# Where late rows of y are computed and moved in a one-core attention and mode-mixing kernel

## The chip, the cores and the metric

The kernel runs on one core of one Trainium2 chip. The metric is device time in microseconds (us) of a whole execution. The engines that matter are TensorE (PE, matrix products), VectorE (DVE), ScalarE (ACT), GpSimd (POOL) and SyncE (SP), which issues transfers. Each takes its instructions in a fixed order, and the engines wait for each other by semaphores. TensorE writes to PSUM, from where VectorE and ScalarE read.

## The reference

For eight batches and eight heads of 576 positions by 64, causal attention with a forget gate is computed. Its output, as rows of 512 features, is x. A real Fourier transform of x along the sequence is cut to 64 modes, each mode is multiplied by its own complex 512 x 512 matrix, and the inverse transform gives y. With u = x + y the result is u + relu(u w_ch).

```python
X = np.fft.rfft(x, axis=1)
Yr = np.einsum('bmd,mde->bme', Xr, w_r) - np.einsum('bmd,mde->bme', Xi, w_i)
Yi = np.einsum('bmd,mde->bme', Xr, w_i) + np.einsum('bmd,mde->bme', Xi, w_r)
y = np.fft.irfft(Y, n=S, axis=1)
u = x + y
return (u + np.maximum(u @ w_ch, 0.0)).astype(np.float32)
```

The mode matrices are 64 x 2 x 512 x 512 values in float32, far more bytes than the rest of the inputs.

## The kernel before

The features are split into four chunks of 128 (`dc`). In the first part of the kernel the attention of all heads of a chunk is computed batch by batch, its output goes into `x_all`, and a product with a basis gives the modes of x (`XT3`). Beside it the mode matrices are loaded, by transfers that POOL issues at line 86, as tiles of four modes: `wb` holds both matrices of four modes for one chunk, 1 MB as they arrive, in a ring of nine buffers. There are 4 x 16 = 64 mode tiles. `emit_modes(n)` multiplies one with the modes of x (32 matmuls of 16 columns at line 111) and adds the result to the sum over chunks in VectorE (line 122, or 126 for the last chunk).

For the last chunk the tiles are taken in a turned order, so that the modes 0 to 15 come last, as tiles 60 to 63 (`GL` is 4). The other 48 modes end in `YT`, in which the places of modes 0 to 15 are zero; the late 16 modes end in `YTl`. Only the last tile's load is cut into two halves of modes, each with a transfer for either matrix: four transfers of 256 KB instead of two of 512 KB. Its matmuls take the first half's modes first.

What the output needs of a batch are two matrices in `yy`: the mode rows transposed to lie with modes on partitions (index 0), and the same times `w_ch` (index 1). Each has 128 rows, a real and an imaginary one for each mode; rows 0 to 31 are the late modes. `emit_y(b)` computes both for one batch from `YT`: four matmuls of 512 columns into `pyw` (line 596) and four transposes into `yp` (line 606), which ScalarE (603) and VectorE (609) copy to `yy`. It writes the late rows too, as zeros. `emit_late(q4)` does the same for the late modes of four batches at once, from `YTl`, into one PSUM tile `pl` (lines 644 and 648): the four batches' late rows stand under each other, 32 each, and eight copies of 32 rows (lines 658 and 659, VectorE and ScalarE) move them to rows 0 to 31 of `yy`. The two copies of a batch read the same `pl`, and are made to follow each other.

Outputs are written by 24 jobs: for each batch, rows 0 to 255, rows 256 to 511, and rows 512 to 575. `emit_x` opens a job with products with the identity matrix, which put x (`pu`, line 667) and x times w_ch (`pz`, line 672) into PSUM. `emit_out` adds the inverse transform by products with the basis `BI` (line 684, two for each of `pu` and `pz`, one in a job of 64 rows), then ends the job in one of two ways. A job of rows 256 to 511, the first job and the last one copy `pu` on ScalarE (L700) and take the maximum and add on VectorE (L701). The others leave x out of `pu`, add it on VectorE (L694), take the maximum on ScalarE (L697) and add on POOL (L698). Then SP issues the store (L707, or L705 for 64 rows).

`pu`, `pz`, `pl` and the last mode tile's sum all use the pool `psZ`: four PSUM buffers of two banks. A buffer is free again when the last reader of its tile is done.

The order before the last tile is set by a loop that takes tiles up to 62, and after the tiles 60, 61 and 62 emits two, two and four batches of y. Then `emit_x` of the first job, tile 63, `emit_late(0)` and the jobs follow in program order, with `emit_late(1)` in front of job 3. A scheduler then sets each engine's order from priorities and free buffers, so that neighbours in the program can change places: in the built program the copies of `pl` already stand one by one between the evictions of the first outputs.

## Time and profile before

| | us |
|---|---|
| median of 7 runs | 469.97 |
| the runs | 468.49, 468.57, 468.59, 469.97, 470.22, 470.35, 470.75 |
| profiled execution | 468.59 |
| its span, first to last instruction | 466.6 |
| TensorE busy | 324.7 (70%) |
| VectorE busy | 251.0 (54%) |
| ScalarE busy | 250.8 (54%) |
| GpSimd busy | 123.5 (26%) |
| weight transfers (POOL's queue), share of 16 engines | 86.9% |
| mean granted TensorE clock | 0.802 |

Times in the profile are counted from the first instruction. "L111" is a line of the kernel file. An arrow in square brackets names what ended an engine's idle time before an instruction. The chain of work that ended last is followed back from the last instruction, at each step to what released it. A stage is read by what ends last in it: an engine that is idle there costs nothing.

### The profile page before, as it was taken

How to read it: one execution, taken by the hardware profiler on the slowest of the kernel's cores; microseconds unless marked ns; L12 is line 12 of the kernel's file. 1: busy time of each engine (PE TensorE's matmuls, PEld its weight loads, DVE VectorE, ACT ScalarE, POOL GpSimd, SP SyncE). 2: the span in 40 equal slices, each digit the busy share in tenths (PEclk: the TensorE clock that was granted, in tenths of full speed). 3: DMA queues.
4: the chain of work that ended last, by engine and by line, in shares of the span. 5: the costliest groups of instructions: out<-in, count | busy, mean ns of one | idle time of the engine just before them, and what ended most of it. 6: DMA issues, size and time to landing. Idle time of an engine off the chain costs nothing.

```text
span 466.6 us, 11413 instructions
## 1 busy us (share of the span) xinstructions
PE 324.7 (70%) x4800; PEld 237.9 (51%) x4845; DVE 251.0 (54%) x625; ACT 250.8 (54%) x376; POOL 123.5 (26%) x154
## 2 busy tenths in 40 slices
PE   1667778995666556566556656776379999688994
PEld 1445556774555445455435545665345655454341
DVE  6767898994544444554444446555223233235774
ACT  4779999995544444555445446553013444135763
POOL 6111100411222222131222222232232323200794
PEclk9979999997575776667667567586559999689998
DMA  9999999999999999999999999999999999991577
GB/s 206 269 267 268 268 268 268 267 269 255 226 236 236 236 236 229 233 231 236 230 230 236 236 226 207 206 207 206 206 207 206 207 207 206 207 163 63 188 287 277
DMA packets 93235, 106.27 MB, mean 228 GB/s; under 512 B 4032, under 2 KB 88512, under 8 KB 93184
## 3 DMA queue, kind: packets, MB, share of 16 engines
q0 software_dynamic: 68144, 67.64, 86.9%
q1 hardware_dynamic: 25040, 37.90, 25.4%
q8 instruction: 38, 0.62, 0.5%
q14 instruction: 13, 0.11, 0.1%
HBM read 163.73 MB, written 9.44 MB: 371 GB/s over the span
## 4 chain that ended last, share of the span: by engine, by line
DMA 74%; PE 9%; ACT 8%; DVE 5%; issue 2%; DVEq 0%; POOL 0%; SPq 0%; ACTq 0%
DMA wb<-in_moe_w_i_dram 70%; ACT E L437 3%; DMA stv<-in_v_dram 3%; PE pz L672 2%; PE pu L684 2%; ACT KTz L384 2%; PE pz L684 1%; ACT uo L700 1%; DVE vb L366 1%; PE pyw L596 1%; DMA Yacc<-in_f_dram 1%; DVE E L452 1%; PE pu L667 1%; PE tp L375 1%; PE A L111 1%
## 5 line engine op out<-in xcount | busy, mean ns | idle before, releaser
L111 PE MATMUL A<-XT,wb 128*128 128x16 bf16 x2048 | 75.6, 172 | 93.3 <-DMA wb<-in_moe_w_i_dram 81.6
L111 PEld LDWEIGHTS <-wb 128*128 128x128 bf16 x2048 | 67.7, 100 | 108.1 <-DMA wb<-in_moe_w_i_dram 90.0
L437 ACT ACTIVATE E<-ps 128x1024 bf16<-128x1024 f32 (+1 forms) x128 | 108.1, 871 | 24.0 <-PE ps L430 22.1
L86 POOL DMA_DIRECT2D wb<-in_moe_w_r_dram x65 | 48.4, 745 | 186.0 <-DMA wb<-in_moe_w_r_dram 86.3
L384 ACT COPY KTz<-tp 64x576 bf16<-64x576 bf16 x64 | 41.3, 645 | 81.7 <-PE tp L375 80.9
L430 PE MATMUL ps<-QTs,KTz 128*128 128x64 bf16 (+4 forms) x353 | 75.9, 315 | 5.8 <-ACT E L437 4.9
L86 POOL DMA_DIRECT2D wb<-in_moe_w_i_dram x65 | 48.3, 743 | 117.8 <-DMA wb<-in_moe_w_i_dram 114.0
L464 PE MATMUL pav<-va,E 128*128 128x65 bf16 x960 | 54.2, 217 | 9.7 <-PE px L488 3.5
L464 PEld LDWEIGHTS <-E 128*128 128x128 bf16 x960 | 48.6, 114 | 13.0 <-issue 5.8
L122 DVE TENSOR_TENSOR Yacc<-A,Yacc 128x256 f32<-128x256 f32 x32 | 14.1, 439 | 63.1 <-PE A L111 62.5
L591 ACT CAST XW<-pxw 128x512 bf16<-128x512 f32 x40 | 22.8, 587 | 39.9 <-PE pxw L584 39.7
L452 DVE TENSOR_TENSOR E<-E,trimask 128x256 bf16<-128x256 bf16 (+2 forms) x128 | 37.6, 300 | 12.0 <-ACT E L437 11.2
L430 PEld LDWEIGHTS <-KTz 128*128 128x128 bf16 x384 | 34.4, 112 | 11.9 <-issue 7.4
L584 PE MATMUL pxw<-wch,yy 128*128 128x512 bf16 x152 | 37.4, 396 | 1.9 <-DVE yy L580 1.6
L366 DVE TENSOR_TENSOR vb<-stv,wdec 96x768 bf16<-96x768 f32 x32 | 30.1, 941 | 5.1 <-DMA stv<-in_v_dram 5.1
L698 POOL TENSOR_TENSOR uo<-uo 64x512 f32<-64x512 f32 (+1 forms) x14 | 25.1, 1809 | 28.9 <-DVE uo L694 27.5
L473 DVE TENSOR_TENSOR x_all<-pav,rcp 128x384 bf16<-128x384 f32 x64 | 31.0, 485 | 0.4
L496 DVE CAST XT<-px 128x128 bf16<-128x128 f32 x32 | 23.2, 725 | 13.3 <-PE px L488 13.0
L126 DVE TENSOR_TENSOR YT<-A,Yacc 128x256 bf16<-128x256 f32 x12 | 7.4, 613 | 42.2 <-PE A L111 42.2
L360 ACT CAST kb<-stk 96x768 bf16<-96x768 f32 x32 | 26.7, 835 | 0.7 <-DMA stk<-in_k_dram 0.7
L584 PEld LDWEIGHTS <-yy 128*128 128x128 bf16 x160 | 15.3, 102 | 21.5 <-DVE yy L580 6.0
L488 PE MATMUL px<-bas,x_all 128*128 128x128 bf16 x160 | 24.4, 261 | 2.4 <-DVE x_all L473 1.1
(101 smaller groups left out, 474.9 us busy)
## 6 DMA issues: line engine op xcount, KB each, us to landing
wb<-in_moe_w_r_dram POOLq DMA_DIRECT2D x63, 512.0 KB, 24.1
wb<-in_moe_w_i_dram POOLq DMA_DIRECT2D x63, 512.0 KB, 25.0
stq<-in_q_dram SPq DMA_DIRECT2D x32, 288.0 KB, 8.7
stk<-in_k_dram SPq DMA_DIRECT2D x32, 288.0 KB, 9.0
stv<-in_v_dram SPq DMA_DIRECT2D x32, 288.0 KB, 9.8
out_dram<-uo SPq DMA_DIRECT2D x16, 512.0 KB, 3.0
out_dram<-uo SPq DMA_DIRECT2D x8, 128.0 KB, 2.6
wch<-in_moe_w_ch_dram POOLq DMA_DIRECT2D x1, 512.0 KB, 37.9
```

Of the source, the lines that this page charges most:

```text
L86: nc.gpsimd.dma_start(wb[:, t, ms, :], src[g * MG : (g + 1) * MG, dc * 128 : (dc + 1) * 128, :][ms].rearrange("m p e -> p m e"),)
L111: nc.tensor.matmul(A[:, eb, mi, :], lhsT=wb[:, t, mi, eb * 128 : (eb + 1) * 128], rhs=XT3[:, m, c0 : c0 + 2 * B], start=(t == 0), stop=(t ...
L360: nc.scalar.copy(kv, stk_[:, :, :, :])
L366: nc.vector.tensor_tensor(vb[:, :, :, :], stv_[:, :, :, :].rearrange("p h r d -> p r h d"), _strided(wdec6[:, 0, c0 : c0 + 1], [[BH, NR], ...
L384: nc.scalar.copy(KTz[s % NK][h][hs, 0:S].rearrange("c (p r) -> c p r", r=NR), tv[hs, :, :],)
L430: nc.tensor.matmul(ps[:, h, o : o + n], lhsT=KTz[s % NK][h][:, jb * 128 : (jb + 1) * 128], rhs=QT[s][:, jb * 128 + c0 : jb * 128 + c0 + n] ...
L437: nc.scalar.activation(E[:, :, piece * 512 : piece * 512 + w], ps[:, :, 0:w], ACT.Exp, scale=scale,)
L452: nc.vector.tensor_tensor(dg, dg, tr, ALU.mult)
L464: nc.tensor.matmul(pav[:, i, h, :], lhsT=E[:, h, c : c + 128], rhs=va[:, jb, h, :], start=(jb == 0), stop=(jb == sb),)
L473: nc.vector.tensor_tensor(x_all[:, b, sbs[0] : sbs[0] + n, dc * 128 : (dc + 1) * 128].rearrange("p c (h d) -> p c h d", h=2), pav[:, 0:n, ...
L584: nc.tensor.matmul(pxw[:, :], lhsT=xT[:, eb, sb * 128 : (sb + 1) * 128], rhs=wch[:, eb, :], start=(eb == 0), stop=(eb == NDC - 1),)
L698: nc.gpsimd.tensor_tensor(o_sb, o_sb, u_sb, ALU.add)
```

## The change

It has three parts. After the tiles 60, 61 and 62 the loop emits three, three and one batches of y, and one more follows behind the loop. The rows of `pl` are moved by a new function, `emit_rows`, one batch at a time: batch 0 after `emit_late(0)`, batches 1 to 3 after the jobs 0, 1 and 2; `emit_late(1)` stands behind job 8 with the rows of batch 4, and batches 5 to 7 follow the jobs 9, 10 and 11. The store of the last job, 64 rows of the last batch, is issued by ScalarE's queue.

```diff
                 if nmode > last - GL:
-                    for _ in range((2, 2, 4)[nmode - (last - GL) - 1]):
+                    for _ in range((3, 3, 1)[nmode - (last - GL) - 1]):
                         emit_y(ny)
                         ny += 1
-            assert nx == ny == B
+            emit_y(ny)
+            assert nx == B == ny + 1
...
-            for i in range(4):
-                b = 4 * q4 + i
-                rows = slice(32 * i, 32 * i + 32)
-                nc.vector.tensor_copy(yy[0:32, b, 0, :], ply[rows, :])
-                nc.scalar.copy(yy[0:32, b, 1, :], plw[rows, :])
+            return ply, plw
+
+        def emit_rows(b, pl):
+            rows = slice(32 * (b % 4), 32 * (b % 4) + 32)
+            nc.vector.tensor_copy(yy[0:32, b, 0, :], pl[0][rows, :])
+            nc.scalar.copy(yy[0:32, b, 1, :], pl[1][rows, :])
...
             if nb == 1:
-                nc.sync.dma_start(out[b, 512:576, :], uo[:Ms, 1, 0, :])
+                eng = nc.scalar if b == B - 1 else nc.sync
+                eng.dma_start(out[b, 512:576, :], uo[:Ms, 1, 0, :])
...
-        emit_late(0)
+        pl = emit_late(0)
+        emit_rows(0, pl)
         for n, job in enumerate(jobs):
-            if n == 3:
-                emit_late(1)
             emit_out(*job, emit_x(*job) if n else ps0)
+            if n == 8:
+                pl = emit_late(1)
+                emit_rows(4, pl)
+            if n in (0, 1, 2, 9, 10, 11):
+                emit_rows(n + 1 if n < 3 else n - 4, pl)
```

## The prediction

> **What bounds the kernel now.** I read the chain that ended last first, then the timeline from 395 us to the end, then the busy time and DMA share by window.

> ```profile
> DMA 74%; PE 9%; ACT 8%; DVE 5%; issue 2%; DVEq 0%; POOL 0%; SPq 0%; ACTq 0%
> ```
> ```profile
> 395.91 20.05 DMA wb<-in_moe_w_i_dram
> 415.97 0.05 issue
> 416.01 0.94 PE A L111 x31
> ...
> 421.09 0.22 PE yp L606 x4
> 421.31 0.43 PE pu L667 x2
> 421.74 0.02 issue
> 421.76 0.59 PE pz L672 x2
> 422.35 0.81 PE A L111 x32
> 423.16 0.02 issue
> 423.18 0.62 DVE YTl L126
> ```

> The page's shares say that weights arriving from memory set the pace for three quarters of the span. The chain shows where this stops: mode tile 62 lands at 415.97, and from 416.01 the chain is TensorE alone: tile 62, four batches of y, the four opening matmuls of output 0, tile 63. So the question is when tile 63 could have run.

> ```profile
> 406.08 0.71 POOL L86 DMA_DIRECT2D wb<-in_moe_w_i_dram  x1 [1.82 <-DMA wb<-in_moe_w_i_dram]
> ```
> ```profile
> wb<-in_moe_w_i_dram POOLq DMA_DIRECT2D x1, 256.0 KB, 15.0
> ```

> This is the last weight transfer (timeline, and DMA issues of 406.0 to 406.5, the last column being us to landing): issued at 406.08, landed at 421.1. The other three quarters of tile 63 landed at 417.2, 418.5 and 419.9 by the same view. TensorE came to tile 63 only at 422.19, 1.1 us after all of it was there.

> The stage from 423 us on is 24 output jobs. Its beat is the copy of `pu` at L700, once in three jobs (timeline, start and duration first):

> ```profile
> 427.87 1.01 ACT L700 COPY uo<-pu 128x1024 f32<-128x1024 f32 x1
> ...
> 430.23 0.38 PE L644 MATMUL pl<-ident_bf,YTl 128*128 128x128 bf16 x4 [0.70 <-ACT uo L697]
> ...
> 433.73 1.01 ACT L700 COPY uo<-pu 128x1024 f32<-128x1024 f32 x1
> ...
> 438.47 1.01 ACT L700 COPY uo<-pu 128x1024 f32<-128x1024 f32 x1
> ...
> 442.96 1.01 ACT L700 COPY uo<-pu 128x1024 f32<-128x1024 f32 x1 [0.70 <-PE pu L684]
> ```

> The further beats are 446.86, 450.71, 454.60 and 458.50: 3.885 us each (15.54 over four). A batch's 17 matmuls of 512 columns at 0.2155 take 3.66 of that, so TensorE sets this stage too. The first three intervals are 5.86, 4.74 and 4.49: together 3.43 over the beat. That is what the late rows cost: 1.25 us of `pl` matmuls for the second four batches (430.23 to 431.48), and waits around the row copies.

> The end is three stores on SP (timeline) and the DMA share and GB/s (last columns by window):

> ```profile
> 460.88 0.89 SPq L707 DMA_DIRECT2D out_dram<-uo  x2
> 461.86 0.72 SPq L705 DMA_DIRECT2D out_dram<-uo  x1
> ```
> ```profile
> 462.00:463.00 1.00, 0.00 (x0) 0.00 (x0) 0.00 (x0) 0.00 (x0) 0.00 (x0) 0.80 1.06 408
> 463.00:464.00 1.00, 0.00 (x0) 0.00 (x0) 0.00 (x0) 0.00 (x0) 0.00 (x0) 0.50 1.05 408
> 464.00:465.00 1.00, 0.00 (x0) 0.00 (x0) 0.00 (x0) 0.00 (x0) 0.00 (x0) 0.50 0.80 285
> ```

> They land 2.8, 3.6 and 3.4 us after their issues at 460.88, 461.4 and 461.86, so at 463.7, 465.0 and 465.3; the DMA engines are full to about 464.8. The span closes at 466.6.

> **Part 1, y before the last tile.** In the built order two batches, not one, stand between tiles 62 and 63: one in the loop, one after it. Three stand behind tile 60 and three behind tile 61. No instruction is added; no weight transfer is moved, the last having been issued at 406.08. Step by step:
> - Third y behind tile 60: in the old run tile 61 starts at 410.91. A y takes 2.1 us at the granted clock of 0.50 and 1.08 at 1.00 (4 x 0.2155 + 4 x 0.054); the window 410 to 412 has a mean clock of 0.65, so it changes near 411.4. The third y then ends near 412.2, tile 61 (0.9) near 413.1.
> - Three y behind tile 61: 3.24, to 416.35. Tile 62 starts there, 0.34 after its old 416.01, and ends at 417.25. This takes the place of the 1.9 us in which TensorE waited.
> - Two y (2.16), to 419.4; opening matmuls of output 0 (421.09 to 422.19 in the old run, 1.10), to 420.5; first half of tile 63, 16 matmuls at 0.027, to 420.95. Then it waits for the last weights: 421.1 + 0.05, 15 matmuls (0.40) and the last one's 0.17: VectorE can add at 421.7, against 423.18.
> So 1.48 us, not the 2.16 of two y: the transfer takes the place of the rest. The y that the words of the change leave out costs nothing, covered by that wait with 0.15 to spare; without the cover (landing at 420.6 or earlier) the gain is at most 2.0, and it is nothing if the weights land at 422.6. The last transfers of tiles 60 to 62, issued at 385.74, 390.79 and 395.91, landed 20.1 later by the same view: with tile 63 the landings stand 5.1 apart (405.8, 410.9, 416.0, 421.1). So I keep 1.5; ends 1.0 and 2.0.

> On VectorE and ScalarE the y evictions (0.42 and 0.59 per batch) run beside 1.08 of TensorE each: nothing.

> **Part 2, rows of y.** All 16 row copies (VectorE 0.42, ScalarE 0.58) and both `pl` groups remain. In the old built order the copies of the first group already stood between the evictions of outputs 0 to 3; the new order swaps only the fourth VectorE copy with the 0.68 us eviction of output 2. What moves is the second group: its matmuls from behind output 2 to behind output 8, its copies to one per output up to 13, in the same pattern as before. SP and POOL issue the same work in the same order. Its `pl` holds one of four PSUM buffers (`psZ`) from its transposes to its last row copy: 430.2 to 440.1 in the old run, about as long in the new.
> I laid the rows' durations along both orders (an instruction starts when its engine is free and its inputs are there). The old order then gives beats of 5.92, 4.76, 4.40 and 3.81, close to the trace's 5.86, 4.74, 4.49 and 3.89; the new one 5.14, 3.82, 4.83, 4.70, 4.39 and 3.81. Over the beat that is 3.65 old and 3.84 new: the second group pays its 1.25 of TensorE and some 1.2 of waits wherever it stands, the first group's rows pay 1.3 by themselves, and what the two shared in the first interval (0.2) is gone. I take +0.2. Ends: -1.0, if those 1.2 of waits hide (VectorE has 0.78 idle per beat, 3.885 less two of 1.215 and one of 0.675; ScalarE 1.26); +2.0, if the first group alone still takes the whole 1.98 over the beat of the old first interval, and the second group costs the 3.43 besides.
> [...]

> **Part 3, last store.** ScalarE is idle after its last copy, so nothing is queued behind its new wait for VectorE. The store leaves beside the second one, 0.46 earlier. But 1.18 MB at 408 GB/s is 2.9 us, and the engines were full throughout, so the last byte moves little. Ends: -0.3 (the last landing falls to that of the second store) and +0.5 (an issue on ScalarE as slow as the slowest L705 on SP, 1.66, instead of 0.72, less the 0.46). The first transfer that SP issued, at 0.81, took 0.59 and landed in 3.3, so a queue's first use shows no price. I take -0.1.
> [...]

> **Sum.** -1.5 + 0.2 - 0.1 = -1.4. Against the profiled execution (468.59: span 466.6 and 2.0 around it) that is 467.2. The seven runs form two groups, three at 468.5 to 468.6, with the profiled one, and four at 470.0 to 470.8; the median 469.97 is in the upper. From the median: 468.6.

> **Rivals.**
> - Gain given back in the output stage: part 2 at its +2.0 end. For: `pl` holds a buffer longer per row. Against: same pattern, same work. 469.0 against the profiled run, 470.4 from the median.
> - Slower: the held buffer starves TensorE in the steady stretch, where all outputs but one in three go through POOL. Each of the three beats over which the second `pl` is held pays the 1.98 of the worst old one: 5.9 instead of 2.5, +3.4, net +1.8 with the other parts: 471.8 from the median. It decides from 2.9 on, which is the 1.5 won and 1.4 (0.3%) more. Against: the old hold cost 0.86 and 0.60 after its first beat.
> - Weights hide it: tile 63 lands 1 us later or more beside TensorE's order. Gain 0.5 or less: 469.5. Against: the even 5.1.
> - More: landing at 420.6 and rows that hide, 2.0 + 1.0 + 0.3: 466.7.

> **How the numbers follow.** 0.3% is 1.4 us, about what a measurement of this kernel can tell from no change, and the forecast lies on that line. Forecast 0.60, more 0.12, given back 0.12 and hidden by weights 0.08, slower rival 0.08. The median after may fall into either group (1.8 apart). Of the forecast's 0.60, three in seven fall low and are faster, of the rest half: 0.43 faster, 0.17 within. The 0.12 are faster. Of the 0.20 given back or hidden, 0.05 faster, 0.12 within, 0.03 slower; of the 0.08, 0.01 within, 0.07 slower. Range 466.6 to 470.4: the low group with a gain of 1.9, up to the gain given back.

> **What would show it.** Tile 63's second half should wait on the last `in_moe_w_i` transfer, and its VectorE add start near 421.7. The L700 beats should be near 5.1, 3.9, 4.8, 4.7, 4.4, then 3.9. The last store should issue beside the second, with the DMA share at 1.0 to the end. I am wrong if TensorE finds tile 63 late or early by over 0.5 us, or if the beats with the second group exceed 5.5.

## The result, and the profile after

| | before | after |
|---|---|---|
| median, us | 470.15 (47 runs) | 467.23 (19 runs) |
| lowest and highest | 468.43 to 472.15 | 466.87 to 468.79 |
| profiled execution | 468.59 | 468.63 |
| its span | 466.6 | 466.5 |

The ratio is 0.9947, with an interval of 0.9935 to 0.9958: about 2.5 us faster, and 2.9 by the medians. The profiled executions, though, stand level. So two things have to be explained: why the profile shows nothing, and why the medians show twice the forecast gain.

The chain of the kernel after around the last mode tile (start, duration, what):

```profile
406.21 15.01 DMA wb<-in_moe_w_i_dram
...
421.27 0.55 PE A L111 x15
...
421.84 0.62 DVE YTl L126
...
422.95 1.29 PE pl L649 x3
424.24 0.85 PE pu L669 x2
```

The timeline has the waits of the same two instructions:

```profile
421.27 0.54 PE L111 MATMUL A<-XT,wb 128*128 128x16 bf16 x15 [0.55 <-DMA wb<-in_moe_w_i_dram]
421.84 0.60 DVE L126 TENSOR_TENSOR YTl<-A,Yacc 128x256 bf16<-128x256 f32 x1 [2.11 <-PE A L111]
```

The chain now goes straight from the last weight transfer, landed at 421.22, to the last 15 matmuls of tile 63 and to VectorE's add. Before, it went through four batches of y, and the add began 2.10 us after the landing (423.18 against 421.08); here 0.62 after (421.84). Yet three matmuls of `pl` take 1.29 us, where three took 0.81 before (timeline of before):

```profile
424.29 0.81 PE L648 MATMUL pl<-wch,YTl 128*128 128x512 bf16 x3
```

The busy time by window (PE, PEld, DVE, ACT and POOL, then granted TensorE clock, DMA share, GB/s) says why:

```profile
422.00:423.00 1.00, 0.45 (x5) 0.38 (x7) 0.45 (x1) 0.00 (x0) 0.00 (x0) 1.00 0.06 16
423.00:424.00 1.00, 1.00 (x3) 0.35 (x3) 0.00 (x0) 0.00 (x0) 0.00 (x0) 0.57 0.00 0
...
426.00:427.00 1.00, 1.00 (x4) 0.35 (x3) 0.00 (x0) 0.99 (x1) 0.00 (x0) 0.72 0.00 0
```

From 423.15 to 426.56 the granted clock is 0.50. The profiled execution of before had no such stretch here; its window is

```profile
423.00:424.00 1.00, 0.30 (x9) 0.21 (x6) 0.61 (x1) 0.00 (x0) 0.00 (x0) 1.00 0.08 16
```

What part 1 won was spent on it, in this one execution.

The copies of `pu` in the output stage (timeline; now L702):

```profile
427.62 1.01 ACT L702 COPY uo<-pu 128x1024 f32<-128x1024 f32 x1
432.79 1.01 ACT L702 COPY uo<-pu 128x1024 f32<-128x1024 f32 x1
436.64 1.01 ACT L702 COPY uo<-pu 128x1024 f32<-128x1024 f32 x1 [0.27 <-PE pu L686]
441.26 1.01 ACT L702 COPY uo<-pu 128x1024 f32<-128x1024 f32 x1
445.99 1.01 ACT L702 COPY uo<-pu 128x1024 f32<-128x1024 f32 x1
```

The next copies are at 450.51, 454.41 and 458.26. The beats are 5.17, 3.85, 4.62, 4.73 and 4.52, then 3.90 and 3.85: the second group of rows now makes a hump in the middle, where before the first three beats held everything.

The last stores (timeline), and what the DMA engines moved there (windows as above):

```profile
460.74 0.89 SPq L710 DMA_DIRECT2D out_dram<-uo  x2
461.15 0.56 ACTq L708 DMA_DIRECT2D out_dram<-uo  x1
```
```profile
462.00:463.00 1.00, 0.00 (x0) 0.00 (x0) 0.00 (x0) 0.00 (x0) 0.00 (x0) 1.00 1.04 395
463.00:464.00 1.00, 0.00 (x0) 0.00 (x0) 0.00 (x0) 0.00 (x0) 0.00 (x0) 1.00 1.07 324
464.00:465.00 1.00, 0.00 (x0) 0.00 (x0) 0.00 (x0) 0.00 (x0) 0.00 (x0) 0.55 0.96 293
```

ScalarE issues its store beside SP's second one, as the change says. The engines are just as busy as before, but move less: 324 GB/s in the second window against 408.

To set executions beside each other I cut each at five points: the landing of the last weight transfer (its issue on POOL plus the time to landing, 15.0), the add at L126, the copy of `pu` in the first job, the same copy in job 22, and the end of the span. These intervals, not the spans, show what a part does, because the landing itself differs between executions by 1.4 us. The labels are those of the runs below.

| execution | landing | to add | to first copy | to job 22 | to end | landing to end |
|---|---|---|---|---|---|---|
| before | 421.08 | 2.10 | 3.05 | 32.27 | 8.10 | 45.52 |
| e9, before again | 421.43 | 2.11 | 3.06 | 32.27 | 8.03 | 45.47 |
| e10, before again, clock fell | 421.26 | 3.78 | 3.06 | 32.26 | 8.04 | 47.14 |
| after, clock fell | 421.21 | 0.63 | 4.14 | 32.28 | 8.24 | 45.29 |
| e8, after again | 421.62 | 0.63 | 3.05 | 32.25 | 8.25 | 44.18 |
| e1, part 1 alone | 421.23 | 0.63 | 3.06 | 32.26 | 8.12 | 44.07 |
| e12, part 1 again, clock fell | 420.95 | 0.63 | 3.99 | 32.44 | 8.09 | 45.15 |
| e2, part 2 alone, clock fell | 422.32 | 3.52 | 3.06 | 32.25 | 8.15 | 46.98 |
| e3, part 3 alone | 421.61 | 2.09 | 3.06 | 32.27 | 8.57 | 45.99 |

### The profile page after: what moved, and what is told of

Read it like the earlier page. It is cut to its first block, busy times and chain, and to the rows that moved or that the text cites. A ratio compares the mean times of both kernels' runs of the same rounds, so it can differ in the third digit from the quotient of the medians.

```text
span 466.5 us, 11413 instructions
## 1 busy us (share of the span) xinstructions
PE 324.1 (69%) x4800; PEld 237.4 (51%) x4845; DVE 251.4 (54%) x625; ACT 250.5 (54%) x376; POOL 123.9 (27%) x154
## 4 chain that ended last, share of the span: by engine, by line
DMA 89%; PE 6%; ACT 1%; issue 1%; DVE 1%; POOL 1%; DVEq 0%; ACTq 0%; POOLq 0%
DMA wb<-in_moe_w_i_dram 69%; DMA wb<-in_moe_w_r_dram 12%; DMA wch<-in_moe_w_ch_dram 8%; PE pz L674 2%; PE pu L686 2%; PE pz L686 1%; ACT uo L702 1%; PE pu L669 1%; ACT uo L699 0%; PE pl L649 0%; POOL wb L86 0%; DVE uo L703 0%; DVE uo L696 0%; DVEq L755 0%; PE pl L645 0%
## 5 line engine op out<-in xcount | busy, mean ns | idle before, releaser
L111 PE MATMUL A<-XT,wb 128*128 128x16 bf16 x2048 | 75.7, 172 | 94.8 <-DMA wb<-in_moe_w_i_dram 82.5
L111 PEld LDWEIGHTS <-wb 128*128 128x128 bf16 x2048 | 67.6, 100 | 109.9 <-DMA wb<-in_moe_w_i_dram 90.9
L86 POOL DMA_DIRECT2D wb<-in_moe_w_r_dram x65 | 48.5, 747 | 187.9 <-DMA wb<-in_moe_w_r_dram 85.6
L86 POOL DMA_DIRECT2D wb<-in_moe_w_i_dram x65 | 48.6, 747 | 115.6 <-DMA wb<-in_moe_w_i_dram 111.7
L584 PE MATMUL pxw<-wch,yy 128*128 128x512 bf16 x152 | 36.4, 388 | 1.9 <-DVE yy L580 1.6
L700 POOL TENSOR_TENSOR uo<-uo 64x512 f32<-64x512 f32 (+1 forms) x14 | 25.1, 1809 | 28.6 <-DVE uo L696 25.8
L126 DVE TENSOR_TENSOR YT<-A,Yacc 128x256 bf16<-128x256 f32 x12 | 7.3, 612 | 42.1 <-PE A L111 42.1
L390 DVE COPY QTs<-tp 128x576 bf16<-128x576 bf16 x32 | 24.0, 749 | 3.5 <-PE tp L375 3.1
```

The costliest lines, as they stand in the source:

```text
L86: nc.gpsimd.dma_start(wb[:, t, ms, :], src[g * MG : (g + 1) * MG, dc * 128 : (dc + 1) * 128, :][ms].rearrange("m p e -> p m e"),)
L111: nc.tensor.matmul(A[:, eb, mi, :], lhsT=wb[:, t, mi, eb * 128 : (eb + 1) * 128], rhs=XT3[:, m, c0 : c0 + 2 * B], start=(t == 0), stop=(t ...
L584: nc.tensor.matmul(pxw[:, :], lhsT=xT[:, eb, sb * 128 : (sb + 1) * 128], rhs=wch[:, eb, :], start=(eb == 0), stop=(eb == NDC - 1),)
L700: nc.gpsimd.tensor_tensor(o_sb, o_sb, u_sb, ALU.add)
```

## The experiments

The theory at the outset was that of the prediction: part 1 saves the time from the landing to the add and nothing else. The rival, formed on seeing the profile after, was that the granted clock makes the rest of the difference, by falling in most executions of before and in few of after.

**Each part alone.** The first run takes part 1 alone:

```diff
-                    for _ in range((2, 2, 4)[nmode - (last - GL) - 1]):
+                    for _ in range((3, 3, 1)[nmode - (last - GL) - 1]):
...
-            assert nx == ny == B
+            emit_y(ny)
+            assert nx == B == ny + 1
```

> Only the y batches are moved (three, three, one and one); rows and store as before. First theory (the weights' landing ends the gain, 1.5 us; what came on top of it, some 1.1 us in the median, is TensorE's clock: without the 1.9 us wait in front of tile 62 the clock falls to half less often in the last 50 us): the lowest runs at 467.0 and most runs near them, median 467.1 to 467.6. Second theory (the clock has no part; rows and store gave the other 1.1): every run 1.5 lower than before's, so a median near 468.7 and two groups as before.

It took 467.13 (12 runs), ratio 0.9955, interval 0.9937 to 0.9972, beside 470.0 for before in the same comparison. One of the runs was at 470.31, the others at 468.44 or below. That is the whole gain of the change. In the table, 1.47 us goes between landing and add, and nothing comes back later.

The second takes part 2 alone, the rows (the kernel after, with these lines put back and the last store on SP again):

```diff
-                    for _ in range((3, 3, 1)[nmode - (last - GL) - 1]):
+                    for _ in range((2, 2, 4)[nmode - (last - GL) - 1]):
...
-            emit_y(ny)
```

> Only the late rows are moved one batch at a time and the second group is put behind output 8. First theory: +0.2 us, median 470.2 to 470.4, runs spread as before's. Second theory: 0.5 to 1.1 us faster, median 469.1 to 469.7.

It took 470.16, ratio 1.0012, interval 0.9997 to 1.0027. There is no gain, and no loss that can be told from none. From the first copy to job 22 it needs 32.25 us, with beats of 5.14, 3.86, 4.61, 4.73 and 4.53; before needs 32.27.

The third takes part 3 alone:

```diff
-                nc.sync.dma_start(out[b, 512:576, :], uo[:Ms, 1, 0, :])
+                eng = nc.scalar if b == B - 1 else nc.sync
+                eng.dma_start(out[b, 512:576, :], uo[:Ms, 1, 0, :])
```

> Only the last store goes to ScalarE's queue. First theory: -0.1 us (between -0.3 and +0.5), as the three last stores fill the transfer engines whoever issues them. Second theory: up to -0.5 us.

It took 469.75, ratio 1.0008, interval 0.9991 to 1.0026: the total says nothing. The profile says a little more. From job 22's copy to the end it took 8.57 us, where all profiles with the store on SP took 8.03 to 8.15. With the rows moved too the store on ScalarE took 8.24 to 8.30; why that is less than 8.57 is not shown. The DMA issues of the kernel with this part alone show what became of the transfers (median us from issue to landing last):

```profile
out_dram<-uo SPq DMA_DIRECT2D x1, 512.0 KB, 4.4
out_dram<-uo ACTq DMA_DIRECT2D x1, 128.0 KB, 3.9
```

These are the two that go out side by side, at 461.87 and 461.92. In before the same 512 KB landed 3.6 us after its issue and the 128 KB 3.4 after:

```profile
out_dram<-uo SPq DMA_DIRECT2D x1, 512.0 KB, 3.6
```

It is so in the kernel after and in e8 too, with the small store on ScalarE (4.4 us for the large one), and in e1 and e11, with it on SP (3.6 us). With the small store beside it, the large one took 0.8 us longer to land.

One thing about these two runs stays open. None of the 24 executions of part 2 or part 3 alone was below 469.2, while 10 of the 35 of before beside them were. The later end accounts for at most 0.5 us of that in part 3; for part 2 the profile shows nothing that does.

**The clock.** TensorE waits for tile 62 in the profiled execution of before and in the run of before again that lasted 470.34 us (timelines, in this order):

```profile
416.01 0.94 PE L111 MATMUL A<-XT,wb 128*128 128x16 bf16 x31 [1.88 <-DMA wb<-in_moe_w_i_dram]
```
```profile
416.21 0.93 PE L111 MATMUL A<-XT,wb 128*128 128x16 bf16 x31 [1.99 <-DMA wb<-in_moe_w_i_dram]
```

In the second the windows around tile 62 are:

```profile
414.00:415.00 1.00, 0.21 (x5) 0.09 (x2) 0.42 (x1) 0.59 (x1) 0.00 (x0) 1.00 1.21 207
415.00:416.00 1.00, 0.00 (x0) 0.00 (x0) 0.00 (x0) 0.00 (x0) 0.00 (x0) 1.00 0.82 133
416.00:417.00 1.00, 0.79 (x32) 0.80 (x33) 0.00 (x0) 0.00 (x0) 0.00 (x0) 1.00 0.72 117
417.00:418.00 1.00, 1.00 (x10) 0.44 (x7) 0.61 (x1) 0.00 (x0) 0.00 (x0) 0.81 0.68 113
418.00:419.00 1.00, 1.00 (x7) 0.64 (x6) 0.25 (x1) 0.59 (x1) 0.00 (x0) 0.50 0.61 100
```

TensorE stands still from 414.2 to 416.2, waiting for tile 62, and the clock then is 0.50 from 417.61 to 421.02. The chain of the same execution shows the price: one batch of y takes 1.71 us for its four wide matmuls, the next only 1.01.

```profile
418.72 1.71 PE pyw L596 x4
...
420.85 1.01 PE pyw L596 x4
```

In the first two rows of the table, before without such a fall, the stretch from landing to end is 45.5 us; with it, 47.14. So a fall costs 1.65 here, close to the 1.8 between the two groups of before's runs. To test this as a cause, and not only see it beside the time, eight matmuls whose result nobody reads were put into the wait of before, ahead of tile 62:

```diff
+                    if nmode == last - 2:
+                        pf = psBig.tile([128, D], F32, tag="big", name="pf")
+                        for i in range(8):
+                            nc.tensor.matmul(
+                                pf[:, :], lhsT=ident_bf[:, :], rhs=wch[:, 0, :],
+                                start=True, stop=True,
+                            )
```

> The kernel before, with eight matmuls of 512 columns added behind the two y batches that follow tile 61, into a PSUM tile that nobody reads: 1.72 us of work in the 1.9 us in which TensorE waited for tile 62. First theory (clock): the lowest runs stay at 468.5, but most runs are now there, median 468.5 to 469.0, faster with work added. Second theory: the added work is hidden or costs up to 0.2 us, median 470.1 to 470.4, two groups as before.

More work made it faster: 468.87, ratio 0.9983, interval 0.9971 to 0.9995, and none of its 12 runs was above 469.33, while of before's 35 runs beside it 25 were at 469.42 or more. In the timeline the filler ends at 415.5, the wait that is left is 0.25 us, and the window of the clock stays at 1.00:

```profile
413.66 1.89 PE L628 MATMUL pf<-wch,ident_bf 128*128 128x512 bf16 x8
...
415.81 0.93 PE L111 MATMUL A<-XT,wb 128*128 128x16 bf16 x31 [0.25 <-DMA wb<-in_moe_w_i_dram]
```
```profile
417.00:418.00 1.00, 1.00 (x9) 0.61 (x8) 0.51 (x2) 0.34 (x1) 0.00 (x0) 1.00 0.63 104
```

**The y that stands in front of tile 63.** The prediction costed at nothing the y that the words of the change leave out. One more y was moved forward, so that only one stands there:

```diff
-                    for _ in range((3, 3, 1)[nmode - (last - GL) - 1]):
+                    for _ in range((4, 3, 0)[nmode - (last - GL) - 1]):
```

> The changed kernel with four, three and none in the loop, so that really one batch of y stands between tiles 62 and 63. Landing theory (tile 63's last transfer sets the start of the output stage): TensorE only waits longer for it, 1.1 us instead of 0.55; the lowest runs stay at 466.9, and the median is 467.2 or, if the longer wait lets the clock fall more often, up to 467.8. Order theory (each y taken out of the way is worth its 1.08): lowest runs at 465.8 to 466.4.

It took 468.28 (5 runs), ratio 0.9945, interval 0.9926 to 0.9963: not faster than the change itself. The median lies above the 467.2 to 467.8 that the landing theory gave. Three of the five runs were at 468.3 to 468.6, and the profiled one of them has the fall of the clock, from 423.01 to 426.42. The timeline:

```profile
421.19 0.54 PE L111 MATMUL A<-XT,wb 128*128 128x16 bf16 x15 [1.09 <-DMA wb<-in_moe_w_i_dram]
421.76 0.60 DVE L126 TENSOR_TENSOR YTl<-A,Yacc 128x256 bf16<-128x256 f32 x1 [2.83 <-PE A L111]
```

The wait for the weights is 1.09 us long instead of 0.55, and the add begins 0.62 after the landing, as in the kernel after. The transfer takes the place of the y, and the order theory, which wanted runs at 465.8 to 466.4, had none below 467.16.

**Filling the new order's waits.** In the kernel after, unread matmuls were put into three waits: two ahead of tile 62, two between the halves of tile 63, three ahead of `emit_late(0)`'s transposes:

```diff
+            if mi == FM and late.get("pl") is not None:
+                emit_fill(late["pl"][:, 0, :], 2)
...
+                    if nmode == last - 2:
+                        pf = psBig.tile([128, D], F32, tag="big", name="pf")
+                        emit_fill(pf[:, :], 2)
...
+            if q4 == 0:
+                emit_fill(plw, 3)
```

> The changed kernel with matmuls that nobody reads in its three waits: two in front of tile 62, two between the halves of tile 63, three between tile 63 and the late rows (0.43, 0.43 and 0.65 us). Clock theory: no run is helped that had a full clock, so the lowest stay at 466.9 to 467.0, but the scatter above 467.7 (a quarter of the runs of the changed kernel) goes; median 467.1. Rival (the scatter is from the transfers): lowest 0 to 0.2 higher and the scatter unchanged.

It took 467.55 (6 runs), ratio 0.9945, interval 0.9929 to 0.9961: not better than the change, and two runs were still above 467.7 (467.86 and 468.72), so that the clock theory's expectation was missed. The clock did not fall in its profile, but the add began 0.85 us after the landing instead of 0.63: the two matmuls between the halves stand in the way when TensorE comes late. The next run also cuts the last tile at three modes instead of two, so that fewer matmuls wait for the last transfers:

```diff
-        parts = 2 if n == NDC * NG - 1 else 1
-        for h in range(parts):
-            ms = slice(h * MG // parts, (h + 1) * MG // parts)
+        cuts = ((0, 3), (3, MG)) if n == NDC * NG - 1 else ((0, MG),)
+        for m0, m1 in cuts:
+            ms = slice(m0, m1)
...
-    FM = MG // 2
+    FM = 3
```

> As the run with matmuls in three waits, and the last weight tile is cut into three modes and one instead of two and two, so that 7 instead of 15 matmuls are left when the last transfer lands. Landing theory: 8 x 0.027 = 0.21 us less, lowest runs at 466.7, median 466.9. Rival (something else sets the start, or a transfer of 128 KB that is issued as late lands no earlier and the larger one lands later): 0 to 0.3 slower than without the cut.

It took 467.23 (6 runs), ratio 0.994, interval 0.9921 to 0.9958, with the lowest run at 466.99; the landing theory had given 466.9 and 466.7. The add began 0.50 after the landing. One run of six was still at 468.73. With them ran the change once more, as it is:

> The changed kernel once more, on the same chip as the three others: median 467.1 to 467.4, lowest 466.9; a second profile of it, in which the output stage starts 1.5 us before the old one, and which ends near 465.1 if the clock stays at 1.00 from 412 us on.

It took 467.56 (4 runs), ratio 0.9941, interval 0.9921 to 0.9962, 0.2 above the expected. Its profile is one of after without the fall: from landing to end 44.18 us, against 45.29 in the profile shown above. So a fall costs 1.1 in the new order, where the work that it slows is the late rows and the first outputs.

**Before, twice more.** One execution each, to have profiles of before with and without the fall:

> The kernel before once more, for a second profile. Clock theory: if its time is 469.8 or more, the clock falls to 0.50 for some 3 us behind TensorE's wait in front of tile 62, and from the landing of tile 63 to the last chunk's last add it takes 3.5 us instead of 2.1; if its time is 468.8 or less, the clock stays at 1.00 there. Rival (the weights arrive later in the slow runs): the landing of tile 63 is 1.2 to 1.8 later than 421.1, and the 2.1 stays.

It took 468.88, and the clock did not fall.

> The kernel before a third time, for one more profile; each theory expects the same of it as of the second.

It took 470.34, and the clock fell; the windows are shown above. The rival, weights that arrive later in the runs of the upper group, does not hold here: the last landing was at 421.26, not later than the 421.43 of the faster one, and from landing to add it took 3.78.

**A version of what was learned.** Part 1 alone, the last tile cut at three modes, and three unread matmuls only where TensorE waits for the add at L126 anyway:

```diff
+        cuts = ((0, 3), (3, MG)) if n == NDC * NG - 1 else ((0, MG),)
...
+            for _ in range(0 if q4 else 3):
+                nc.tensor.matmul(
+                    plw, lhsT=ident_bf[:, :], rhs=wch[:, 0, :], start=True, stop=True
+                )
```

> Only the y part of the change; the last weight tile cut into three modes and one, and three matmuls that nobody reads between tile 63 and the late rows, where TensorE waits 0.66 us for VectorE. Landing theory: the add starts 0.42 instead of 0.63 after the last landing, and with the store on SP the end follows 0.15 sooner: lowest runs at 466.6, median 466.8 to 467.0; the matmuls cost nothing. Rival: as the y part alone, 467.1.

It took 466.95, ratio 0.9935, interval 0.9916 to 0.9953, and all six runs lie from 466.88 to 467.24. This is the lowest median of all, with the least scatter. Timeline and a window:

```profile
421.30 0.33 PE L111 MATMUL A<-XT,wb 128*128 128x16 bf16 x7 [0.35 <-DMA wb<-in_moe_w_i_dram]
421.49 0.81 PE L640 MATMUL pl<-wch,ident_bf 128*128 128x512 bf16 x3
421.67 0.61 DVE L126 TENSOR_TENSOR YTl<-A,Yacc 128x256 bf16<-128x256 f32 x1 [1.91 <-PE A L111]
```
```profile
423.00:424.00 1.00, 1.00 (x5) 0.39 (x4) 0.36 (x1) 0.00 (x0) 0.00 (x0) 1.00 0.00 0
```

Seven matmuls instead of 15 follow the last transfer, the add begins 0.42 after the landing, the filler lies beside it, and the clock at 423 us is 1.00, where the kernel after had 0.57. Beside it part 1 ran again without the two additions:

> The y part alone once more on the same chip as the one with the cut tile: median 467.0 to 467.3. If the cut and the added matmuls help, it is 0.2 us slower than they are.

It took 467.47 (6 runs), ratio 0.9946, interval 0.9928 to 0.9965; three runs at 467.0 and three from 467.9 to 468.4. Its profile, of 467.89, has the fall, and from landing to end 45.15 us, 1.1 more than part 1's first profile. The two intervals overlap, so that the version is faster than part 1 rests on the profiles and the scatter. It differs from part 1 by two things at once, and which of them took the scatter away was not shown.

## Why the prediction was right, and where it was not

**Part 1, -1.5.** Right, by the mechanism and by the number. The last transfer landed at 421.21 for a predicted 421.1, the second half of tile 63 waited for it, and the add began at 421.84 for a predicted 421.7. From landing to add 2.10 became 0.63: -1.47. That the y left out of the words costs nothing was borne out by the run with one y in front of the tile. The cover was larger than predicted: TensorE waited 0.55 us for the last weights, not 0.15, which taken strictly is beyond the 0.5 us that the prediction named as a sign of being wrong. The clock rose at 409.5 in this execution, not near 411.4, so that tile 61 began at 411.38 for a predicted 412.2. In e8, where it rose at 412.2, the wait was 0.2. The gain was the same in both.

**Part 2, +0.2.** The beats were predicted at 5.14, 3.82, 4.83, 4.70, 4.39 and 3.81, and came at 5.17, 3.85, 4.62, 4.73, 4.52 and 3.90. The sum of the six was predicted within 0.1 (26.69 against 26.79). But the forecast did not use the sum: it used the amount over each laid-out order's own beat, and took the old order's from the same working, which gives 26.5 for six beats (5.92, 4.76, 4.40 and three of 3.81), where part 1 alone, with the old row order, shows 26.74 (426.55 to 453.29). The rows cost 26.79 - 26.74 = 0.05 over six beats, and nothing up to job 22. The term was mis-sized by 0.15 to 0.2. Held against the trace's old beats instead of the laid-out ones, it would have come out at -0.05, about as far off on the other side. The measured value lies well inside the bounds. The second group's `pl` was held for 9.9 us in both orders (430.23 to 440.08 before, 437.71 to 447.60 after), so the runs do not show what a longer hold would cost.

**Part 3, -0.1.** The wrong sign, within the bounds that were given. The store did leave about as much earlier as forecast (461.92 is 2.89 after job 22's copy, in before 3.36), but the end came 0.15 to 0.5 later. The step that failed is "the engines were full throughout, so the last byte moves little": the share of busy time was full, the rate was not. From 463 us on the engines moved 324 and 293 GB/s, where before they moved 408 and 285, and the 512 KB store took 4.4 us to land instead of 3.6. What lowered the rate was not shown.

**The sum, -1.4.** Where the clock did not fall, from landing to end 45.52 and 45.47 became 44.18: -1.3. The forecast was right for this stretch. Its errors were 0.15 to 0.2 in part 2 and, the other way, 0.25 to 0.3 in part 3, and cancel in part. From span to span it shows less, because e8's last weights landed 0.5 us later than those of before.

**The median, 468.6.** It came at 467.23, which is the time that the prediction gave for its low group, and inside its range. Group against group the forecast holds: before's 14 runs below 469.1 have a median of 468.56, after's 16 below 468 one of 467.21, a gain of 1.35. What failed is the sentence "the median after may fall into either group": the group was treated as chance that stays three in seven whatever the order. In before it is the clock: the run with the filler took the upper group away (none of its 12 executions was above 469.33). The fall then cost 1.65, and in the new order it costs 1.1. Of before's 47 runs 14 were below 469.1; of after's 19 only three were above 468 (468.14, 468.41, 468.79). Of the 2.9 by medians 1.3 is the path; the other 1.6 would be the fall, if it came less often. That it does is argued from these times and not shown: only the profiled executions show the clock of this stretch, and of those without added matmuls three of five with the new order of y had the fall (after, e5, e12), against two of five with the old order (e2, e10). Nor does a single time decide it, for e12's execution of 467.89 had the fall and e8's of 467.83 had not. So 1.6 us of the gain by medians is something that the prediction had only as chance, and that its range held the result is in part luck.

**The rivals.** Given back in the output stage: no, 32.27 and 32.28 or 32.25. Slower by the held buffer: no, the beats with the second group are 4.52 to 4.73, not 5.9. Hidden by the weights: no, the landings of after were 421.2 and 421.6, not 422.1 or later. More: no, neither an earlier landing nor hidden rows.

Three things stay open: how often the clock falls in the new order; why the filled version of before (468.87) and the last version (466.95) are 1.9 apart, while landing to add explains 1.5 of it (1.91 to 0.42); and why e6 and e7, whose profiles have no fall, each still had one run at 468.7.

## What to carry to other kernels

Before moving work in front of a wait, find the transfer that the wait ends on: the gain is the time from its landing to the work that needs it, not the work moved (here 1.47 of 2.16 us). When equal runs form two groups, take profiles of both and compare the granted clock first; here a wait of TensorE of 1.99 us stood in front of a fall of the clock that cost 1.65, and with eight matmuls that nobody reads in that wait none of 12 runs was in the upper group.

## What was unexpected of the hardware

Standing still alone does not decide it. Laid on this grid from 409 to 432 us, the steps in front of the five falls hold 1.24 to 1.99 us of it, while steps that kept the clock hold up to 1.31 (e9, 412.60 to 416.01). The two kinds differ in TensorE's other work than the matmuls of 16 columns at L111: at most 1.06 us of it in the steps in front of a fall, at least 1.27 in all others. In after's step, 419.74 to 423.15, TensorE is busy for 2.11 us, of which L111 has 1.11; in before's, 414.80 to 418.22, for 2.21, of which L111 has 0.94. Where between these the border lies, and whether it is this work that decides, no run tested.

The time from issue to landing of a 512 KB store grew from 3.6 to 4.4 us when a store of 128 KB left beside it on another engine's queue instead of 0.47 us later on the same one, though the DMA engines were as busy without it (a share of 1.05 from 463 to 464 us in before, 1.07 in after).
